# Four PSUM banks as one tile, v loaded and cast by GpSimd, and state by head pairs, in a fused RWKV and squared-ReLU kernel

## Chip, cores and metric

The kernel runs on one core of one Trainium2 chip. The metric is the device time in microseconds (us) of one execution. Three runs of the kernel before gave 177.93, 178.39 and 179.38 us; the median is 178.39 us.

The engines have short names in what follows: PE is TensorE (PEld its weight load), DVE is VectorE, ACT is ScalarE, POOL is GpSimd, SP is SyncE, which here only issues transfers. PSUM, into which PE writes, has eight banks; a bank holds 512 float32 values in each of 128 partitions.

## What is computed

```
def _attn_ref(r, k, v, w, u):                       # r, k, v: (4, 8, 768, 48); w, u: (8, 48)
    state = np.zeros((B, H, D, D), dtype=np.float32)
    for t in range(S):
        kt, vt, rt = (k[:, :, t].copy(), v[:, :, t].copy(), r[:, :, t].copy())
        cur = np.einsum('bhd,bhe->bhde', u[None] * kt, vt)
        y[:, :, t] = np.einsum('bhd,bhde->bhe', rt, state + cur)
        state = w[None, :, :, None] * state + np.einsum('bhd,bhe->bhde', kt, vt)
...
x = y as (3072, 384) tokens
h = x @ w_in                                        # w_in: (384, 2048)
g = np.maximum(h, 0.0) ** 2
out = g @ w_out                                     # w_out: (2048, 384)
```

First comes a linear attention with a decaying state (batch 4, 8 heads, 768 steps, head size 48), then two matrix products with a squared ReLU between them on its output.

## The kernel before

**Units.** The 768 steps are cut into 6 chunks of 128; a chunk of one batch is a unit, so there are 24 units (`units`, chunk outermost). Inside a unit the recurrence is written as matrices. r and k are multiplied by powers of w (`scale`, L321: tiles `wpos` and `wneg`, made from the logarithm of w at the start), which gives `rkw`. This is transposed to `rkT`: for the first 6 units by PE and ACT (`turn`, `evict_rk`), for the others by a transposing transfer on SP's queue (`turn_dma`, L330). From `rkT` come the scores of 128 by 128 for each head (`at`, L358, PE), which DVE masks and evicts (`mask`, L370). `sums` (PE, L378 and L383) makes the diagonal term from `rk` (the u part) and, in the same bank, the unit's new part of the state. `diag_v` (DVE, L392) multiplies the diagonal term by v. `state_add`, `state_decay` and `state_cast` (L400 to L412) update the state of the batch in float32 and leave a bfloat16 copy `stb`. `y_mm` (PE, L421 and L427) adds masked scores times v and r times the state; `evict_y` (DVE, L436) evicts this as `yb`, and it is transposed into `xT` (`x_turn` or `x_dma`).

**The two products.** `mm1` (PE, L468) multiplies `xT` by w_in, into one bank for each 512 values; a group takes one unit, or two units for six pairs in the middle (`GROUPS`), so that its matmuls are 128 or 256 wide. ACT evicts each bank with a ReLU (`relu`, L476, tile `gr`). The square is taken by ACT (`square`, L483) or DVE (L485), by the letters of `SQUARES` in turn. `mm2` (PE, L492) multiplies by w_out, four calls of four matmuls into one bank for a unit, and ACT evicts (`evict_o`, L499) before the store. The last unit does this in two halves (L508).

**State by heads.** The heads of a pair share the 128 partitions, 64 each. `sums` makes a block of 96 columns for a pair, of which only the two diagonal blocks are wanted; `state_add` and `state_cast` work on them one by one, in 64 partitions and 192 values each, and `stb` has its other blocks set to zero at the start.

**Order.** Nothing is ordered by the framework: the function declares each step with a cost, its needs, the buffers it takes and a rank (`Plan.add`), and `Plan.run` goes through them in a list schedule with these costs and writes out one program in order of the planned starts. The rank decides between steps that are ready. A PSUM bank is given to a step when the plan starts it (the bank that has been free longest), and fillers (`fill`, L276, matmuls of a constant) go into PE's queue where the plan has nothing for it in the first 16 us. The planned times are not in the program. What an engine waits for in the end are semaphores that are put in from the tiles that each instruction reads and writes: an instruction waits for those that stand before it in the written order and touch the same tile in a conflicting way. For PSUM two reads of a bank by two engines are also kept apart.

**Transfers.** Loads of r, k and v, the transposes and the stores go by SP's queue, in the plan's order; a transfer's semaphore is used again after eight transfers of its kind, and the later one waits for the earlier. The weights go by GpSimd's queue, which casts them to bfloat16; a one-element copy (`weights`, L306) that reads a loaded tile holds each of them back (`FRONT`). w is loaded once into all 128 partitions by ACT's queue, and once with u by GpSimd for the columns.

Of the kernel before, what the change touches and what calls it, by code (L numbers as in the profile page):

```python
# [16 lines left out]
class Plan:  # L17
# [9 lines left out]
    def __init__(self, lags, cold, spare):  # L27
        self.lags = lags
        self.cold = cold
        self.spare = spare  # L30
        self.steps = []
        self.at = {}
        self.users = {}
        self.place = {}

    def add(self, key, engine, cost, emit, needs=(), rank=0.0, new=(), uses=(), move=None):
        s = dict(key=key, engine=engine, cost=cost, emit=emit, rank=rank, new=new, move=move)
        s["needs"] = [n for n in needs if n is not None]
        self.at[key] = s
        self.steps.append(s)  # L40
        for x in tuple(new) + tuple(uses):
            self.users.setdefault(x, []).append(s)

    def run(self, room, banks, count):
# [10 lines left out]
        begin, until, tight, loose = self.spare  # L55
        held[0] = "spare"
        order = []
        t = 0.0
# [5 lines left out]
        def ready(s, e):  # L64
            if s["move"]:
                return s["end"] + moved
# [96 lines left out]
def kernel(  # L163
# [33 lines left out]
    loads = ctx.enter_context(tc.tile_pool(name="loads", bufs=6))  # L197
# [5 lines left out]
    banks = [psum.tile([128, 512], F32, name=f"bank{n}") for n in range(8)]  # L203
    plan = Plan((0.9, 0.0, 0.2, 0.33, 0.12), (5.5, 1.9), (1.25, 16.0, 0.057, 0.08))
# [20 lines left out]
    nc.vector.memset(warm, 1.0)  # L225
    wu = const.tile([HP, 2, 2, 64], F32)
# [3 lines left out]
    nc.gpsimd.dma_start(out=wu[:, 1, :, :D], in_=u.rearrange("(p o) d -> p o d", o=2))  # L230

# [6 lines left out]
    ident4 = const.tile([HP, HP], F32)  # L238
    make_identity(nc, ident4)
    lnw = const.tile([128, dm], F32)  # L240
# [3 lines left out]
    for wx, by in ((wpos, up), (wneg, down)):  # L244
        nc.scalar.activation(wx.rearrange("p h d -> p (h d)"), lnw, AF.Exp, scale=by)
# [4 lines left out]
    for n in range(NPAD):  # L250
        for x in range(2):
            nc.vector.memset(rkw_b[n][:, x, :, :, D:], 0.0)
# [8 lines left out]
    st32 = [const.tile([128, HP, D], F32, name=f"st32_{b}") for b in range(B)]  # L261
    stb = [const.tile([128, HP, 2 * D], BF16, name=f"stb_{b}") for b in range(B)]
    for b in range(B):
        nc.vector.memset(stb[b], 0.0)

    wend_c = const.tile([128, HP], F32)
    wend = wend_c.unsqueeze(2).to_broadcast([128, HP, D])
# [27 lines left out]

    def load(i, name):
        c, b = units[i]
        src = {"rt": r, "kt": k, "vt": v}[name]
        x = loads.tile([C, H, D], F32, name=name)
        nc.sync.dma_start(  # L300
            out=x, in_=src[b, :, c * C : (c + 1) * C, :].rearrange("h s d -> s h d")
        )
# [19 lines left out]

    def cast_v(i):
        tiles[i]["vb"] = work.tile([C, H, D], BF16, name="vb")
        nc.scalar.copy(tiles[i]["vb"], tiles[i]["vt"])  # L325

    def turn_dma(i):
        t = tiles[i]
        t["rkT"] = work.tile([128, 2, HP, C], BF16, name="rkT")
# [5 lines left out]
    def turn(i, x):  # L335
        t = tiles[i]
        t["tp", x] = bank("h", i, "rk", x).bitcast(BF16)[:, : HP * C].rearrange("p (a c) -> p a c", a=HP)
        if x == 0:
            t["rkT"] = work.tile([128, 2, HP, C], BF16, name="rkT")
# [54 lines left out]
    def state_add(i):  # L394
        c, b = units[i]
        for o in range(2):
            sl = slice(o * 64, o * 64 + 64)
            x = tiles[i]["s"][sl, :, o * D : (o + 1) * D]
            if c == 0:
                nc.vector.tensor_tensor(st32[b][sl], x, wend[sl], ALU.mult)  # L400
            else:
                nc.vector.tensor_tensor(st32[b][sl], x, st32[b][sl], ALU.add)  # L402
# [138 lines left out]
    add("w", ACT, 3.9, None, rank=-1e3)  # L541
    add("wk", ACT, 0.48, None, rank=-1e3, needs=["w"])
    copy("begin", SP, 0.74, None, rank=-1e3)
    add("wu", POOL, 4.6, None, rank=-1e3)
# [3 lines left out]
    add("wend", ACT, 0.4, end_columns, rank=10, needs=["copied"])  # L548
    for n, (what, q, gated) in enumerate(FRONT):
        copy(  # L550
            (what, q), POOL, 1.0, do(weights, gated, q, what), rank=n,
            move=((2.35, 98, 1.25, 0.0) if what == "I" else (2.05, 78, 1.25, 0.0)), needs=[gated], uses=[gated],
        )
    for i in range(NU):
# [4 lines left out]
        for n, name in enumerate(("rt", "kt", "vt")):  # L559
            copy(  # L560
                (name, i), SP, 0.55, do(load, i, name), rank=rank + 0.1 * n, move=(1.06, 16, 0.67, 1.0),
                new=[(name, i)],
            )
        for x in range(2):
# [5 lines left out]
        add(  # L570
            ("vb", i), ACT, 0.405, do(cast_v, i), rank=a + 0.5, needs=[("vt", i), ("rkT", i) if i < 24 else ("scale", i, 1)],
            new=[("vb", i)], uses=[("vt", i)],
        )
# [12 lines left out]
        else:  # L586
            copy(("rkT", i), SP, 1.24, do(turn_dma, i), rank=a - 30, needs=both, move=(1.5, 26, 0.67, 1.0), new=[("rkT", i)], uses=[("rkw", i)])
# [10 lines left out]
        for o in range(2):  # L598
# [7 lines left out]
            new=[("s", i)], uses=[("rk", i), ("rkw", i)] + ([("vb", i)] if c < NCH - 1 else []),  # L606
        )
        add(("dv", i), DVE, 0.465, do(diag_v, i), rank=a + 2, needs=[("sums", i), ("vb", i)], new=[("dv", i)], uses=[("s", i), ("vb", i)])
        if c < NCH - 1:
            add(  # L610
                ("sadd", i), DVE, 0.68, do(state_add, i), rank=a + (4 if c else 3.2),
                needs=[("sums", i), ("stb", before) if c else "wend"], uses=[("s", i)],
            )
            if c > 0:
                add(("sdec", i), DVE, 0.27, do(state_decay, i), rank=a + 4 + 4, needs=[("sadd", i)])
            add(
                ("stb", i), ACT, 0.71, do(state_cast, i), rank=a + 6 + 4,
# [5 lines left out]
            new=[("y", i)], uses=[("am", i, 0), ("am", i, 1), ("vb", i), ("rkT", i)],  # L623
# [8 lines left out]
        else:  # L632
            copy(("xT", i), SP, 1.2, do(x_dma, i), rank=a - 30, needs=xneed, move=(0.6, 26, 0.67, 0.4), new=xnew, uses=[("yb", i)] + xuse)
    begun = 0
    step = 0
    for m in GROUPS:
# [17 lines left out]
        for j in range(i, i + m):  # L654
            a = 4 * j
            squares = [[("sq", i, s) for s in range(q * m, q * m + m)] for q in range(NQ)]
            if j < NU - 1:
# [7 lines left out]
                copy(("out", j), SP, 0.42, do(store, j), rank=a + 4 + L2, needs=[("osb", j)], move=(0.58, 75, 0.67, 0.13), uses=[("osb", j)])  # L665
                continue
            for n in range(2):
# [9 lines left out]
                copy(("out", j, n), SP, 0.42, do(store_half, j, n), rank=a + 4 + L2, needs=[("osb", j, n)], move=(0.35, 75, 0.67, 0.13), uses=[("osb", j, n)])  # L677
    room = dict(
        rt=6, kt=6, vt=6, rkw=NPAD, g=2, rkT=4, vb=4, rk=4, am=8, dv=4, yb=4, xT=3, gr=6, osb=6,
    )  # L680
    for s in plan.run(room, dict(at=4, s=2, y=2, h=5, o=2), len(banks)):
# [32 lines left out]
```

## Time and profile before

| | us |
|---|---|
| median of 3 runs | 178.39 |
| profiled execution: its time | 179.7 |
| profiled execution: its span | 177.9 |
| PE busy | 167.5 |
| of it fillers | 11.9 |
| DVE busy | 128.7 |
| ACT busy | 128.8 |
| POOL busy | 11.4 |

The span is the time from the first to the last recorded instruction; 1.8 us of the profiled execution lie around it. A matmul's recorded time contains its way through the array, so that of 12 matmuls of 0.219 us that follow each other only about 0.056 us each are spent; a group's sum of busy time counts overlapping records once. In the rows by line, "mean ns of one" is the length of one instruction, and what stands behind the second bar is the time that the engine sat idle just before the instructions of that row, with what ended most of this. A stretch's row gives, after the length, the busy time of PE, PEld, DVE, ACT and POOL (instructions begun in it), then the clock granted to PE, the transfer engines' share and GB/s.

### The profile page before, as it was taken

What the parts mean: (1) busy time and instruction counts of PE and PEld (TensorE: products, weight loads), DVE (VectorE), ACT (ScalarE), POOL (GpSimd) and SP (SyncE); (2) the same over time, 40 slices, a digit from 0 to 9 for tenths busy, and PEclk for the clock granted to TensorE, in tenths of its full rate; (3) what the DMA queues carried; (4) which work ended last, traced back from release to release, by engine and by line L of the source; (5) the groups of instructions that cost most, each with busy time, mean ns of one, the idle gap of its engine ahead of it and who ended that gap; (6) DMA issues with size and microseconds to landing.
All of it is one profiled execution on the core that took longest, in us unless ns stands there. A gap on an engine that the chain in (4) does not pass through costs nothing.

```text
span 177.9 us, 5106 instructions
## 1 busy us (share of the span) xinstructions
PE 167.5 (94%) x2080; PEld 135.2 (76%) x2080; DVE 128.7 (72%) x279; ACT 128.8 (72%) x268; POOL 11.4 (6%) x35
## 2 busy tenths in 40 slices
PE   7699689999999999989979999899999999999993
PEld 7599479977786886876776796786795797878762
DVE  3389996565989899769779698589598695853100
ACT  2738889999385985597488599488597499659820
POOL 7120950000000000000000000000000000000000
PEclk9999999999999999999999999999999999999999
DMA  5999999999797888869879889999998897940212
GB/s 103 192 179 181 163 197 197 208 190 179 93 208 128 169 155 171 175 132 206 174 161 185 176 166 191 133 201 185 163 199 172 187 201 135 314 135 0 71 67 90
DMA packets 107385, 29.05 MB, mean 163 GB/s; under 512 B 101985, under 2 KB 106849, under 8 KB 107361
## 3 DMA queue, kind: packets, MB, share of 16 engines
q1 hardware_dynamic: 104976, 25.37, 75.1%
q0 software_dynamic: 2240, 3.15, 10.0%
q8 instruction: 16, 0.26, 0.6%
q10 hardware_dynamic: 144, 0.20, 0.6%
q14 instruction: 9, 0.07, 0.1%
HBM read 20.65 MB, written 4.72 MB: 143 GB/s over the span
## 4 chain that ended last, share of the span: by engine, by line
PE 57%; DMA 18%; DVE 17%; issue 3%; ACT 2%; SPq 1%; ACTq 0%
PE bank L492 22%; PE bank L468 22%; DMA rkT<-rkw 8%; DMA rt<-in_r_dram 5%; DVE am L370 4%; DVE rkw L321 4%; DVE yb L436 3%; PE bank L358 3%; DMA xT<-yb 2%; PE bank L276 2%; DMA wrow<-in_w_dram 2%; DVE dv L392 2%; DVE g L485 2%; PE bank L421 1%; PE bank L508 1%
## 5 line engine op out<-in xcount | busy, mean ns | idle before, releaser
L468 PE MATMUL bank<-xT,w_in_q 128*128 128x128 bf16 (+1 forms) x864 | 71.8, 237 | 0.5 <-ACT xT L456 0.3
L476 ACT ACTIVATE gr<-bank 128x512 f32<-128x512 f32 x96 | 55.0, 601 | 19.5 <-PE bank L468 18.9
L468 PEld LDWEIGHTS <-w_in_q 128*128 128x128 bf16 x864 | 64.4, 114 | 3.3 <-issue 0.7
L492 PE MATMUL bank<-w_out_q,g 128*128 128x384 bf16 x368 | 65.1, 326 | 0.0
L492 PEld LDWEIGHTS <-g 128*128 128x128 bf16 x368 | 34.4, 98 | 20.0
L370 DVE TENSOR_TENSOR am<-bank,smask 128x512 bf16<-128x512 f32 x48 | 31.8, 684 | 8.2 <-PE bank L358 8.1
L483 ACT ACTIVATE g<-gr 128x512 bf16<-128x512 f32 x60 | 37.3, 639 | 0.6
L485 DVE TENSOR_TENSOR g<-gr 128x512 bf16<-128x512 f32 x36 | 24.6, 687 | 13.1 <-ACT gr L476 13.0
L499 ACT COPY osb<-bank 128x384 f32<-128x384 f32 x23 | 11.0, 484 | 10.1 <-PE bank L492 7.9
L412 ACT CAST stb<-st 64x192 bf16<-64x192 f32 x40 | 14.0, 350 | 5.1 <-DVE st L406 4.4
L350 DVE TENSOR_TENSOR rk<-rkT 128x512 bf16<-128x512 bf16 x24 | 10.1, 422 | 7.7 <-DMA rkT<-rkw 5.6
L321 DVE TENSOR_TENSOR rkw<-rt,wpos 128x384 bf16<-128x384 f32 x24 | 13.2, 552 | 2.5 <-DMA rt<-in_r_dram 1.7
L436 DVE TENSOR_TENSOR yb<-bank,dv 128x384 bf16<-128x384 f32 x24 | 13.3, 555 | 2.3 <-PE bank L427 1.7
L392 DVE TENSOR_TENSOR dv<-vb,bank 128x384 f32<-128x384 bf16 x24 | 13.1, 545 | 2.6 <-PE bank L383 2.6
L321 DVE TENSOR_TENSOR rkw<-kt,wneg 128x384 bf16<-128x384 f32 x24 | 13.2, 551 | 0.6 <-DMA kt<-in_k_dram 0.3
L276 PE MATMUL bank<-warm 128*128 128x128 bf16 x108 | 11.9, 275 | 1.1 <-DVE warm L225 1.1
L358 PE MATMUL bank<-rkT 64*128 64x128 bf16 x192 | 9.8, 222 | 2.8 <-DMA rkT<-rkw 1.9
L325 ACT CAST vb<-vt 128x384 bf16<-128x384 f32 x24 | 12.2, 508 | 0.2
L402 DVE TENSOR_TENSOR st<-bank,st 64x192 f32<-64x192 f32 x32 | 11.3, 352 | 0.2
L358 PEld LDWEIGHTS <-rkT 64*128 64x128 bf16 x192 | 5.5, 96 | 7.5 <-issue 2.9
L276 PEld LDWEIGHTS <-warm 128*128 128x128 bf16 x108 | 9.6, 128 | 1.4 <-DVE warm L225 1.1
L345 ACT COPY rkT<-bank 128x512 bf16<-128x512 bf16 x12 | 6.9, 585 | 4.5 <-PE bank L341 4.5
(54 smaller groups left out, 97.8 us busy)
## 6 DMA issues: line engine op xcount, KB each, us to landing
rt<-in_r_dram SPq DMA_DIRECT2D x24, 192.0 KB, 4.2
kt<-in_k_dram SPq DMA_DIRECT2D x24, 192.0 KB, 4.0
vt<-in_v_dram SPq DMA_DIRECT2D x24, 192.0 KB, 4.4
out_dram<-osb SPq DMA_DIRECT2D x23, 192.0 KB, 2.8
w_in_q<-in_moe_w_in_dram POOLq DMA_DIRECT2D x4, 384.0 KB, 7.2
w_out_q<-in_moe_w_out_dram POOLq DMA_DIRECT2D x4, 384.0 KB, 13.1
rkT<-rkw SPq DMA_TRANSPOSE x18, 3.8
xT<-yb SPq DMA_TRANSPOSE x18, 3.0
```

The source lines that it names most:

```text
L276: nc.tensor.matmul(out=banks[0][:, :128], lhsT=warm, rhs=warm, start=True, stop=True)
L321: nc.vector.tensor_tensor(t["rkw"][:, x, :, :, :D], pair(src), pair(wx), ALU.mult)
L358: nc.tensor.matmul(out=t["at"][o][:, p, :], lhsT=t["rkT"][sl, 1, p, :], rhs=t["rkT"][sl, 0, p, :], start=True, stop=True,)
L370: nc.vector.tensor_tensor(am, t["at"][o], smask.unsqueeze(1).to_broadcast([C, HP, C]), ALU.mult)
L392: nc.vector.tensor_tensor(t["dv"], t["vb"], t["d"].unsqueeze(2).to_broadcast([C, H, D]), ALU.mult)
L412: nc.scalar.copy(stb[b][sl, :, o * D : (o + 1) * D], st32[b][sl])
L436: nc.vector.tensor_tensor(t["yb"], t["y"], t["dv"].rearrange("p h d -> p (h d)"), ALU.add)
L468: nc.tensor.matmul(out=t["h", s][:, a], lhsT=turned, rhs=chunks[c]["xT"][:, n, b : b + m, :], start=(n == 0), stop=(n == NK - 1),)
L476: nc.scalar.activation(t["gr", s], t["h", s], AF.Relu)
L483: nc.scalar.activation(g, x, AF.Square)
L485: nc.vector.tensor_tensor(g, x, x, ALU.mult)
L492: nc.tensor.matmul(out=t["o"], lhsT=chunks[units[i][0]]["g"][:, f, units[i][1], :], rhs=w_out_q[f // 4][:, f % 4, :], start=(f == 0), stop ...
```

## The change

- w's second load goes to four partitions (0, 32, 64 and 96), two heads each, instead of to 128. Its logarithm is taken there, and four matmuls with a row of ones (`spread_log`) spread it over all partitions, each into a bank of its own. The exponentials that make `wpos` and `wneg` read these four banks at once (`power`).
- For this, banks 4 to 7 are slices of one PSUM tile, `four`. After the start they are banks like the others, given out by the plan.
- v of units 6 to 23 is loaded and cast by GpSimd's queue (`load_v`, eight buffers `vc`). Units 0 to 5 keep SP's load and ACT's cast. These transfers stand behind the weights in GpSimd's queue.
- The state is kept with all its 96 columns for a pair. `wend`, the decay over a chunk, is a tile of 128 by 384 with zeros outside the diagonal blocks, which are filled by GpSimd at the start. Add, decay and cast are one instruction each.
- The zeros that pad `rkw` are set by GpSimd for all but two buffers; there are 8 buffers for `rkw` instead of 5, 6 instead of 4 for `rkT`, 7 instead of 6 for the loads.
- `SQUARES` has six of eight on ACT instead of five; the weights' gates differ; a table `TURNS` gives single steps a rank of their own, so that the whole order differs.

```
+    def add(self, key, ...):
+        kind, which = (key[0], key[1] if len(key) == 2 else key[1:]) if isinstance(key, tuple) else ("", key)
+        rank = self.turns.get(kind, {}).get(which, rank)
...
-                                n = min((n for n in held if held[n] is None), key=lambda n: since[n])
+                                n = 4 + x[1] if x[0] == "log" else min((n for n in held if held[n] is None), key=lambda n: since[n])
...
-    NPAD = 5
-    SQUARES = 'AMAMAAAM'
+    NPAD = 8
+    NVB = 8
+    SQUARES = 'AAAMAAAM'
+    TURNS = {
+        "rt": {
+            0: -49.089, 1: -33.297, 10: 12.513, 12: 23.673, ...
+        },
+        ...
+    }
     FRONT = (
-        ("I", 0, ("kt", 1)), ("I", 1, ("kt", 3)), ("I", 2, ("kt", 3)), ("O", 0, ("kt", 3)),
-        ("I", 3, ("kt", 3)), ("O", 1, ("kt", 3)), ("O", 2, ("kt", 3)), ("O", 3, ("kt", 3)),
+        ("I", 0, ("vt", 0)), ("I", 1, ("kt", 2)), ("I", 2, ("vt", 1)), ("O", 0, ("kt", 3)),
+        ("I", 3, ("kt", 4)), ("O", 1, ("kt", 4)), ("O", 2, ("rt", 4)), ("O", 3, ("rt", 4)),
     )
...
-    banks = [psum.tile([128, 512], F32, name=f"bank{n}") for n in range(8)]
+    four = psum.tile([128, 4, 512], F32, name="four")
+    banks = [psum.tile([128, 512], F32, name=f"bank{n}") for n in range(4)] + [four[:, n] for n in range(4)]
...
-    wrow = const.tile([128, dm], F32)
-    nc.scalar.dma_start(out=wrow, in_=w.rearrange("h d -> (h d)").unsqueeze(0).to_broadcast([128, dm]))
+    wrow = const.tile([128, 2 * D], F32)
+    nc.gpsimd.memset(wrow, 1.0)
+    nc.scalar.dma_start(out=wrow[::32], in_=w.rearrange("(a o) d -> a (o d)", o=2))
...
-    for wx, by in ((wpos, up), (wneg, down)):
-        nc.scalar.activation(wx.rearrange("p h d -> p (h d)"), lnw, AF.Exp, scale=by)
...
+    def spread_log():
+        for a in range(HP):
+            sl = slice(a * 32, a * 32 + 1)
+            nc.tensor.matmul(out=four[:, a, : 2 * D], lhsT=ones[sl], rhs=lnw[sl], start=True, stop=True)
+
+    def power(out, by):
+        nc.scalar.activation(out.rearrange("p (a o) d -> p a (o d)", o=2), four[:, :, : 2 * D], AF.Exp, scale=by)
...
+    def end_blocks():
+        for o in range(2):
+            sl = slice(o * 64, o * 64 + 64)
+            nc.gpsimd.tensor_copy(wend[sl, :, o * D : (o + 1) * D], wend_c[sl].unsqueeze(2).to_broadcast([64, HP, D]))
...
+    def load_v(i):
+        c, b = units[i]
+        tiles[i]["vb"] = work.tile([C, H, D], BF16, name="vc", bufs=NVB)
+        nc.gpsimd.dma_start(out=tiles[i]["vb"], in_=v[b, :, c * C : (c + 1) * C, :].rearrange("h s d -> s h d"))
...
     def state_add(i):
         c, b = units[i]
-        for o in range(2):
-            sl = slice(o * 64, o * 64 + 64)
-            x = tiles[i]["s"][sl, :, o * D : (o + 1) * D]
-            if c == 0:
-                nc.vector.tensor_tensor(st32[b][sl], x, wend[sl], ALU.mult)
-            else:
-                nc.vector.tensor_tensor(st32[b][sl], x, st32[b][sl], ALU.add)
+        nc.vector.tensor_tensor(st32[b], tiles[i]["s"], st32[b] if c else wend, ALU.add if c else ALU.mult)
...
     def state_cast(i):
         b = units[i][1]
-        for o in range(2):
-            sl = slice(o * 64, o * 64 + 64)
-            nc.scalar.copy(stb[b][sl, :, o * D : (o + 1) * D], st32[b][sl])
+        nc.scalar.copy(stb[b], st32[b])
...
-        add(
-            ("vb", i), ACT, 0.405, do(cast_v, i), rank=a + 0.5, needs=[("vt", i), ("rkT", i) if i < 24 else ("scale", i, 1)],
-            new=[("vb", i)], uses=[("vt", i)],
-        )
+        if i < NPE:
+            add(
+                ("vb", i), ACT, 0.405, do(cast_v, i), rank=a + 0.5, needs=[("vt", i), ("rkT", i)],
+                new=[("vb", i)], uses=[("vt", i)],
+            )
+        else:
+            copy(("vb", i), POOL, 1.1, do(load_v, i), rank=a + 50, needs=[("kt", i - 1)], move=(1.06, 16, 1.4, 0.0, LATE[0]), new=[("vc", i)])
```

More of the change, by code (lines that the diff above doesn't have):

```diff
@@ L225 @@
     nc.vector.memset(warm, 1.0)
+    ones = const.tile([128, 128], F32)
+    nc.vector.memset(ones, 1.0)
     wu = const.tile([HP, 2, 2, 64], F32)
@@ L249 @@
     rkw_b = [const.tile([128, 2, HP, 2, 64], BF16, name=f"rkw{n}") for n in range(NPAD)]
-    for n in range(NPAD):
-        for x in range(2):
-            nc.vector.memset(rkw_b[n][:, x, :, :, D:], 0.0)
+    for n in range(2):
+        nc.vector.memset(rkw_b[n][:, :, :, :, D:].rearrange("p x a o e -> p (x a o) e"), 0.0)
     identb = const.tile([128, 128], BF16)
@@ L328, in turn_dma @@
         t = tiles[i]
-        t["rkT"] = work.tile([128, 2, HP, C], BF16, name="rkT")
+        t["rkT"] = work.tile([128, 2, HP, C], BF16, name="rkT", bufs=6)
         nc.sync.dma_start_transpose(
@@ L338, in turn @@
         if x == 0:
-            t["rkT"] = work.tile([128, 2, HP, C], BF16, name="rkT")
+            t["rkT"] = work.tile([128, 2, HP, C], BF16, name="rkT", bufs=6)
         for p in range(HP):
@@ L539 @@
     plan.fill = fill
[L541 to L544, printed above, removed]
+    add("w0", ACT, 2.55, None, rank=-1e3)
+    add("log", PE, 0.25, spread_log, rank=-1e3, needs=["w0"], new=[("log", n) for n in range(4)])
+    add("w", ACT, 0.48, do(power, wpos, up), rank=-1e3, needs=["log"], uses=[("log", n) for n in range(4)])
+    add("wk", ACT, 0.48, do(power, wneg, down), rank=-999, needs=["w"], uses=[("log", n) for n in range(4)])
+    add("wu", POOL, 5.8, None, rank=-1e3)
     add("cols", PE, 0.1, spread_columns, rank=-50, needs=["wu"], new=[("h", "cols")])
@@ L547 @@
     add("uwb", POOL, 0.75, u_columns, rank=-200, needs=["copied"])
-    add("wend", ACT, 0.4, end_columns, rank=10, needs=["copied"])
+    add("end", ACT, 0.4, end_columns, rank=0, needs=["copied"])
+    add("wend", POOL, 0.8, end_blocks, rank=1.5, needs=["end"])
     for n, (what, q, gated) in enumerate(FRONT):
@@ L586 @@
         else:
[L587 removed]
+            copy(("rkT", i), SP, 1.24, do(turn_dma, i), rank=a - 30, needs=both, move=(1.5, 26, 0.67, 1.0, LATE[1]), new=[("rkT", i)], uses=[("rkw", i)])
         add(("rk", i), DVE, 0.335, do(rk, i), rank=a + 1, needs=[("rkT", i)], new=[("rk", i)], uses=[("rkT", i)])
@@ L676 @@
                 )
-                copy(("out", j, n), SP, 0.42, do(store_half, j, n), rank=a + 4 + L2, needs=[("osb", j, n)], move=(0.35, 75, 0.67, 0.13), uses=[("osb", j, n)])
+                copy(("out", j, n), SP, 0.42, do(store_half, j, n), rank=a + 4 + L2, needs=[("osb", j, n)], move=(0.35, 75, 0.67, 0.13, 0.0), uses=[("osb", j, n)])
     room = dict(
-        rt=6, kt=6, vt=6, rkw=NPAD, g=2, rkT=4, vb=4, rk=4, am=8, dv=4, yb=4, xT=3, gr=6, osb=6,
+        rt=7, kt=7, vt=7, rkw=NPAD, g=2, rkT=6, vb=6, vc=NVB, rk=4, am=8, dv=4, yb=4, xT=3, gr=6, osb=6,
     )
-    for s in plan.run(room, dict(at=4, s=2, y=2, h=5, o=2), len(banks)):
+    for s in plan.run(room, dict(at=4, s=2, y=2, h=5, o=2, log=4), len(banks)):
         if s["emit"] is not None:
```

127 lines of the change are left out of this document (100 added, 27 removed), and 16 rows, old and new, of the table TURNS.

## The prediction

> **What bounds the kernel now.** I read the summary first, then the chain that ended last, the stretches in time, and last the rows of the tiles that the change touches.
>
> ```profile
> span 177.9 us, 5106 instructions
> ...
> PE 167.5 (94%) x2080; PEld 135.2 (76%) x2080; DVE 128.7 (72%) x279; ACT 128.8 (72%) x268; POOL 11.4 (6%) x35
> ...
> PE   7699689999999999989979999899999999999993
> ...
> PEclk9999999999999999999999999999999999999999
> ...
> PE 57%; DMA 18%; DVE 17%; issue 3%; ACT 2%; SPq 1%; ACTq 0%
> ```
>
> TensorE (PE) is the bound: 94% busy and most of the chain. ACT and DVE are each at 72%, so work taken from them is worth nothing by itself. What can be gained is PE's idle time and its filler matmuls. The stretches show where these lie (length, then PE, PEld, DVE, ACT, POOL busy):
>
> ```profile
> 5.00:10.00 5.00, 3.78 (x36) 3.31 (x36) 2.18 (x5) 3.06 (x7) 0.78 (x4) 1.00 1.21 192
> ...
> 15.00:20.00 5.00, 4.21 (x83) 3.64 (x81) 4.94 (x11) 4.12 (x9) 1.95 (x4) 1.00 0.94 182
> 20.00:25.00 5.00, 3.74 (x72) 3.02 (x70) 4.94 (x12) 4.41 (x10) 4.68 (x11) 1.00 1.09 169
> 25.00:30.00 5.00, 4.93 (x91) 4.58 (x88) 4.00 (x9) 4.90 (x11) 0.00 (x0) 1.00 1.17 197
> ...
> 85.00:90.00 5.00, 3.98 (x57) 3.27 (x57) 3.03 (x8) 2.61 (x5) 0.00 (x0) 1.00 0.93 197
> ...
> 115.00:120.00 5.00, 4.07 (x51) 3.80 (x49) 3.91 (x8) 4.37 (x10) 0.00 (x0) 1.00 0.99 214
> ```
>
> To 25 us DVE is full and PE waits for it; from 25 us PE is full but for a few gaps (1.02 in 85 to 90, 0.93 in 115 to 120, 0.55 in 75 to 85, 0.37 in 125 to 140: 2.9 us; the chain has transposes `rkT<-rkw` there). So from 25 us on, **any wait put into PE's stream is added to the time.** This is why PE's waits matter most below. The rows for prices:
>
> ```profile
> L476 ACT ACTIVATE gr<-bank 128x512 f32<-128x512 f32 x96 | 55.0, 601 | 19.5 <-PE bank L468 18.9
> L483 ACT ACTIVATE g<-gr 128x512 bf16<-128x512 f32 x60 | 37.3, 639 | 0.6
> L370 DVE TENSOR_TENSOR am<-bank,smask 128x512 bf16<-128x512 f32 x48 | 31.8, 684 | 8.2 <-PE bank L358 8.1
> L485 DVE TENSOR_TENSOR g<-gr 128x512 bf16<-128x512 f32 x36 | 24.6, 687 | 13.1 <-ACT gr L476 13.0
> L499 ACT COPY osb<-bank 128x384 f32<-128x384 f32 x23 | 11.0, 484 | 10.1 <-PE bank L492 7.9
> L392 DVE TENSOR_TENSOR dv<-vb,bank 128x384 f32<-128x384 bf16 x24 | 13.1, 545 | 2.6 <-PE bank L383 2.6
> L325 ACT CAST vb<-vt 128x384 bf16<-128x384 f32 x24 | 12.2, 508 | 0.2
> L402 DVE TENSOR_TENSOR st<-bank,st 64x192 f32<-64x192 f32 x32 | 11.3, 352 | 0.2
> ```
>
> **Work on ACT and DVE.** 18 casts of v go: 18 x 0.508 = 9.1 us off ACT. Squares go from 60 on ACT and 36 on DVE to 72 and 24: 12 x 0.639 = 7.7 onto ACT, 12 x 0.687 = 8.2 off DVE. The state add, two of 64x192 (0.73 a pair on the timeline), becomes one of 128x384 (0.545, by `dv`): 20 x 0.18 = 3.6 off DVE; the decay grows from 0.350 to 0.55 (as `rkw<-rt,wpos`, 128x384): 16 x 0.20 = 3.2 on; the state cast from a pair at 0.72 to one at 0.51: 4.2 off ACT. ACT falls to about 123 us, DVE to about 119. Priced at 0: PE's own work hides it; if DVE's 8.6 us all lay in the first 25 us it would be worth that, but only four state adds (0.7) do.
>
> **Start.** Before, w's 192 KB land 3.64 us after issue, Ln takes 0.52, and `wpos` ends at 5.56. After: a memset on POOL that ACT's queue waits for (to 0.95), a w of 1.5 KB, a shorter Ln, four fp32 matmuls that PE's queue waits for (two smaller ones, L281, took 0.49 together), an exponential of the same size (0.6). With the fastest small transfer of this trace (1.5, the last store) `wpos` is ready at 4.3; with 3.64, a full 0.52 and 1.0 of matmuls at 6.8. I take 2.0 for the transfer: 4.8, so **-0.8**, between -1.3 and +1.3. Queued behind PE's wait are the fillers and the first transposes, which need the same result.
>
> **v by GpSimd.** SP issues 18 transfers fewer (median 0.95 each). The same bytes are read, so DMA time is put at 0. POOL's issues took 0.56 (w_out) to 0.77 (w_in, 384 rows); by rows a v of 1024 would take up to 2.1: 10 to 37 us on an engine that is empty from 25 us. With 8 buffers a v is issued as soon as the unit eight earlier is done with its own; only unit 6 is close, since its v stands behind the last w_out (issued 24.2, 14.7 at most to land: 38.9; plus 4.4 for a v: 43.3; in before its matmuls begin at 44.9). 0, up to +3 if cover fails; late next would be PE's `sums` and `y` of unit 6. Deeper pools (rkT 6, rkw 8) and the freed SP queue should take away the 2.9 us of gaps above: **-2.9**, between 0 and -2.9.
>
> **One tile for four banks.** This is the part that decides. Banks 4 to 7 become slices of one tile `four`. I followed each wait in the changed program to the instruction that raises the semaphore to the awaited value. In the program before, no engine waits for another over a bank that it does not use. In the changed one this happens often: 70 waits of PE on ACT or DVE, 63 between ACT and DVE, 63 of these two on PE, where the only thing shared is `four` and the banks differ. One stretch, unit 9 (lines of the changed kernel; m2 is L596, mask L482, `vc` a v that GpSimd loads):
>
> ```
> PE   L572 m1, writes four bank 0, 12 matmuls     raises PE to 908
> ACT  L580 relu, reads four bank 2                waits PE 908        raises ACT to 97
> PE   L490 diag, writes four bank 3               waits ACT 97
> ```
>
> The relu's own matmuls were done earlier, yet it starts only when the next group is through, and PE stands until it ends. A turn like this costs PE: the matmul's tail after the pitch (0.219 - 0.056 = 0.16), 0.03 to the reader's start, the reader, and 0.06 back (`rkT` ends at 21.76, L358 starts at 21.82): 0.85 with a relu (0.60), 0.93 with a mask (0.68), 0.80 with `dv`, 0.73 with `osb`, less the PE work that stands between. With pitches from the chain (m1 0.67 for 12, wide m1 2.62 for 24, m2 0.65 for 4, L358 0.33 for 8) I did this sum for every wait of PE behind the fillers. One reader deep: 33 stalls, 18.3 us. Two deep, where the reader itself waits for the other engine's reader, as `dv` for a relu for a mask: 43 stalls, 26.8 us. Three deep: 49 stalls, 32.5 us. By the same sum the kernel before has 2 stalls, 1.0 us. ACT's and DVE's own queues, which add to this, are left out. I take the middle of two and three deep, 29.6 - 1.0 = **+28.6**, from which 1.5 at the front lies in PE's idle time there: **+27.1**.
>
> **Sum**: 27.1 - 0.8 - 2.9 = +23.4. The profiled execution took 179.7 (span 177.9, 1.8 around it), 1.3 over the median of 178.39. 179.7 + 23.4 = 203.1 for such an execution; about **202** for the median.
>
> **Rivals.**
> - Half-absorbed: PE's queue stands, but DVE and ACT get ahead, so that only single turns remain. For it: both have 50 us of room. Against: 14 of these stalls have no PE work at all in between. 18.3 - 1.0 - 1.5 - 0.8 - 2.9 = +12.1: 190. Chance 0.14.
> - ACT and DVE take turns: with 63 waits between them, late masks and relus also delay `y` and xT. If every second one costs a further 0.6: 31 x 0.6 = 19 on top: 221. For it: DVE is full to 25 us; against: both have room later. 0.12.
> - The other side: the readers have always finished by the time that PE arrives, since relus waited 18.9 us for PE, not PE for them. Then the start and the gaps remain: 178.4 - 3.7 = 174.7. It decides if fewer than some 4 of the turns stall (3.7 / 0.85). Against: the relu above cannot begin until PE has issued its last matmul. 0.05. [...]
> - The clock falls: PE's short stops bring its clock down. If a third of 165 us of PE work ran at half pace: +55 on top: 257. Against: in 20 to 25 us PE was busy 3.74 of 5 and PEclk stayed at 1.00. 0.03. [...]
>
> **Chances.** The forecast 0.66, the rivals 0.14, 0.12, 0.05, 0.03. No change to 1% (about what a measurement of this kernel can tell) lies only at the edge of the other side: faster 0.04, same 0.01, slower 0.95. The range runs from the half-absorbed case (190, less 1) to three deep with half of the second rival's 19 and nothing gained (178.4 + 31.5 + 9.5 = 219): 189 to 219.
>
> **What would show it.** PE's row busy share falls to the low eighties or lower, with idle time before m1, m2 and diag matmuls of tile `four` released by ACT L580 and DVE L482, some 40 times, 0.5 to 0.9 us each; ACT relus on `four` that begin when a matmul of another bank ends; DVE near 119 and ACT near 123 us. `wpos` ends before 5.56. No wait for `vc` but perhaps unit 6. It is wrong if PE stays above 90% busy from 30 us on, or if the lost time is before `vc` or `rkT` transfers.

## The result, and the profile after

The changed kernel takes 217.84 us (median of four runs, 214.92 to 220.25) against 178.54 for the kernel before in the same rounds: a ratio of 1.214, interval 1.201 to 1.228. It is slower by 39 us. The forecast was 202, with a range of 189 to 219. Some executions of a kernel took longer than its others, a slow state; ratios, their intervals and the differences in us below leave these out, while medians and ranges hold all. The profiled execution took 217.9 us, its span is 216.1.

The summary and the chain that ended last, from the page of the kernel after:

```profile
span 216.1 us, 5059 instructions
...
PE 176.4 (82%) x2088; PEld 137.4 (64%) x2088; DVE 121.1 (56%) x236; ACT 125.4 (58%) x242; POOL 29.7 (14%) x63
...
PE   5976786898987786987787987987998786989894
...
PEclk9999998899996999999999999999999999999999
...
PE 62%; DVE 16%; ACT 15%; issue 3%; DMA 1%; POOL 0%; DVEq 0%; ACTq 0%; POOLq 0%
```

PE does much the same work, but its busy share is down from 94% to 82%, and the stops are spread over the whole span: 11 of the 40 slices in the row of PE are at 90% or more, where 32 were before. DVE (121.1 us) and ACT (125.4) did less than before, as worked out, and gained nothing by it. In the chain, transfers fell from 18% to 1%, and ACT rose from 2% to 15%: the program now ends last because PE, ACT and DVE wait for each other. PEclk dips twice (8 8, and later 6), which it did not do in the profiled execution of the kernel before. The four executions had mean clocks of 0.984, 0.969, 0.984 and 1.00; the one at 1.00 still took 214.92 us, so that the clock is worth some 3 us of the 39.

The groups by line of the kernel after (after the counts: busy us, mean ns of one, idle time before, and what ended it), one line for matmuls into own banks and one for the same matmuls into `four`:

```profile
L596 PE MATMUL bank<-w_out_q,g 128*128 128x384 bf16 x240 | 45.4, 329 | 0.0
L572 PE MATMUL four<-xT,w_in_q 128*128 128x128 bf16 (+1 forms) x486 | 44.8, 242 | 13.1 <-ACT gr L580 5.9 <-DVE yb L540 3.1 <-DVE st L508 1.7
L572 PE MATMUL bank<-xT,w_in_q 128*128 128x128 bf16 (+1 forms) x378 | 33.5, 240 | 0.6 <-ACT xT L560 0.6
L596 PE MATMUL four<-w_out_q,g 128*128 128x384 bf16 x128 | 23.9, 325 | 8.1 <-DVE am L482 5.5 <-ACT gr L580 1.4 <-DVE dv L504 1.1
...
L490 PE MATMUL bank<-uwb,rk 128*128 128x8 bf16 x48 | 3.0, 169 | 0.0
L490 PE MATMUL four<-uwb,rk 128*128 128x8 bf16 x48 | 3.0, 167 | 4.1 <-DVE am L482 3.2 <-ACT gr L580 0.9
```

This is the clearest view of the cause. The same line, with the same operands, waits 13.1 us where it writes a slice of `four` and 0.6 where it writes a bank with a tile of its own; for m2 8.1 against 0.0, for the diagonal term 4.1 against 0.0. What ends these waits has nothing to do with the matmul: m2 (L596) never reads what the mask (L482) makes. In the list of PE's waits (us in total, times, longest):

```profile
PE four L572 <- ACT gr L580: 5.9, 10, 1.4
PE four L596 <- DVE am L482: 5.5, 6, 1.4
PE four L490 <- DVE am L482: 3.2, 3, 1.6
PE four L572 <- DVE yb L540: 3.1, 4, 1.3
```

The whole list has 44 waits of PE on ACT or DVE before a matmul of `four`, 32.2 us together, 0.73 each. The readers wait too, for matmuls and for each other:

```profile
ACT gr L580 <- PE four L572: 14.4, 17, 2.2
...
ACT gr L580 <- DVE dv L504: 5.3, 3, 3.2
...
DVE dv L504 <- ACT gr L580: 4.2, 4, 2.1
DVE am L482 <- ACT gr L580: 4.1, 4, 2.6
```

The first of these rows says little, since relus stood 18.9 us for their own matmuls in the kernel before; the other three have no counterpart there.

Last the chain from 113.66 us, in order of time (start, length, what):

```profile
113.66 0.83 PE four L572 x6
114.51 0.61 ACT gr L580
115.12 0.04 issue
115.16 0.83 PE four L572 x6
116.02 0.60 ACT gr L580
116.61 1.04 ACT g L587 x2
```

In the chain six matmuls into `four`, a relu, six matmuls, a relu follow each other, 1.5 us a pair. PE's own rows in this stretch (in brackets the idle time before, and what ended it):

```profile
113.66 0.82 PE L572 MATMUL four<-xT,w_in_q 128*128 128x256 bf16 x6
114.41 0.40 PE L470 MATMUL bank<-rkT 64*128 64x128 bf16 x8
115.16 0.82 PE L572 MATMUL four<-xT,w_in_q 128*128 128x256 bf16 x6 [0.35 <-ACT gr L580]
115.81 0.24 PE L490 MATMUL bank<-uwb,rk 128*128 128x8 bf16 x4
115.92 0.33 PE L495 MATMUL bank<-vc,rkw 128*128 128x96 bf16 x4
116.66 0.82 PE L572 MATMUL four<-xT,w_in_q 128*128 128x256 bf16 x6 [0.41 <-ACT gr L580]
```

Short matmuls into other banks fill a part of each relu's 0.6 us, and PE stands for the rest, 0.35 and 0.41 us.

### The profile page after: what moved, and what is told of

Same layout as the page of the kernel before. It is cut to its first block, busy times and chain, and to the rows that moved or that the text cites. A ratio compares the mean times of both kernels' runs of the same rounds, so it can differ in the third digit from the quotient of the medians.

```text
span 216.1 us, 5059 instructions
## 1 busy us (share of the span) xinstructions
PE 176.4 (82%) x2088; PEld 137.4 (64%) x2088; DVE 121.1 (56%) x236; ACT 125.4 (58%) x242; POOL 29.7 (14%) x63
## 3 DMA queue, kind: packets, MB, share of 16 engines
q1 hardware_dynamic: 86256, 21.83, 55.7%
## 4 chain that ended last, share of the span: by engine, by line
PE 62%; DVE 16%; ACT 15%; issue 3%; DMA 1%; POOL 0%; DVEq 0%; ACTq 0%; POOLq 0%
PE four L572 17%; PE bank L596 15%; PE four L596 10%; ACT gr L580 10%; DVE am L482 7%; PE bank L572 6%; DVE yb L540 3%; DVE st L508 2%; DVE dv L504 2%; PE bank L372 2%; ACT g L587 2%; PE four L470 1%; DMA wrow<-in_w_dram 1%; PE bank L470 1%; ACT rkT L457 1%
## 5 line engine op out<-in xcount | busy, mean ns | idle before, releaser
L580 ACT ACTIVATE gr<-four 128x512 f32<-128x512 f32 x54 | 31.8, 598 | 42.6 <-PE four L572 14.4
L572 PE MATMUL four<-xT,w_in_q 128*128 128x128 bf16 (+1 forms) x486 | 44.8, 242 | 13.1 <-ACT gr L580 5.9
L596 PEld LDWEIGHTS <-g 128*128 128x128 bf16 x368 | 34.5, 98 | 28.7 <-issue 10.2
L596 PE MATMUL bank<-w_out_q,g 128*128 128x384 bf16 x240 | 45.4, 329 | 0.0
L572 PE MATMUL bank<-xT,w_in_q 128*128 128x128 bf16 (+1 forms) x378 | 33.5, 240 | 0.6 <-ACT xT L560 0.6
L596 PE MATMUL four<-w_out_q,g 128*128 128x384 bf16 x128 | 23.9, 325 | 8.1 <-DVE am L482 5.5
L433 POOL DMA_DIRECT2D vc<-in_v_dram x18 | 15.8, 888 | 93.0 <-PE four L531 44.0
L482 DVE TENSOR_TENSOR am<-four,smask 128x512 bf16<-128x512 f32 x27 | 18.5, 690 | 15.7 <-ACT gr L580 4.1
L580 ACT ACTIVATE gr<-bank 128x512 f32<-128x512 f32 x42 | 24.5, 598 | 4.4 <-PE bank L572 4.3
L482 DVE TENSOR_TENSOR am<-bank,smask 128x512 bf16<-128x512 f32 x21 | 14.0, 686 | 9.2 <-PE bank L470 8.1
L428 DVE TENSOR_TENSOR rkw<-rt,wpos 128x384 bf16<-128x384 f32 x24 | 13.1, 551 | 2.0 <-ACT wpos L380 2.0
L516 ACT CAST stb<-st 128x384 bf16<-128x384 f32 x20 | 10.2, 509 | 6.8 <-DVE st L512 6.7
L428 DVE TENSOR_TENSOR rkw<-kt,wneg 128x384 bf16<-128x384 f32 x24 | 13.1, 551 | 0.0
```

The costliest lines, as they stand in the source:

```text
L428: nc.vector.tensor_tensor(t["rkw"][:, x, :, :, :D], pair(src), pair(wx), ALU.mult)
L433: nc.gpsimd.dma_start(out=tiles[i]["vb"], in_=v[b, :, c * C : (c + 1) * C, :].rearrange("h s d -> s h d"))
L482: nc.vector.tensor_tensor(am, t["at"][o], smask.unsqueeze(1).to_broadcast([C, HP, C]), ALU.mult)
L516: nc.scalar.copy(stb[b], st32[b])
L572: nc.tensor.matmul(out=t["h", s][:, a], lhsT=turned, rhs=chunks[c]["xT"][:, n, b : b + m, :], start=(n == 0), stop=(n == NK - 1),)
L580: nc.scalar.activation(t["gr", s], t["h", s], AF.Relu)
```

## The experiments

Two theories stood at the start. **The tile**: nearly all of the loss comes from the waits that one tile for four banks brings. **The order**: the searched ranks, or v by GpSimd, or the start cost as much. When the first runs showed that the rest of the change cost something as well, the later ones took that apart.

**1. A tile for each bank.** The changed kernel with eight tiles; the exponentials become four for each of `wpos` and `wneg`.

```
-    four = psum.tile([128, 4, 512], F32, name="four")
-    banks = [psum.tile([128, 512], F32, name=f"bank{n}") for n in range(4)] + [four[:, n] for n in range(4)]
+    banks = [psum.tile([128, 512], F32, name=f"bank{n}") for n in range(8)]
```

> The changed kernel, order and all, but banks 4 to 7 are four tiles of their own; the start's exponentials read them bank by bank (eight short ones for two). Theory (PE, ACT and DVE stand in turns because a wait is put in for any bank of the shared tile): nearly the whole loss goes, and what is left is the start and the closed gaps: 178.5 - 3.7 + about 1 for the eight exponentials, 174 to 178; PE over 92% busy, clock 1.00 throughout. Rival A (the searched order, or v by GpSimd, or the wider state work is the loss): it stays above 205. Rival B (half and half): 185 to 205.

Measured: 183.72 us (181.55 to 184.83); ratio to the kernel before 1.017, interval 1.009 to 1.026. With the same program otherwise, 35 of the 39 us are gone (217.8 to 182.3). The tile is the cause, and in the profiled execution (181.55 us) PE's row and clock are back; in the other three the mean clock was 0.979 to 0.988 and the time 1.6 to 3.3 us longer:

```profile
PE 166.8 (93%) x2088; PEld 133.1 (74%) x2088; DVE 118.5 (66%) x236; ACT 122.3 (68%) x248; POOL 30.3 (17%) x63
...
PEclk9999999999999999999999999999999999999999
```

But 174 to 178 was expected, and this kernel is 3.3 us above the kernel before (4.7 by the medians of all runs, the figure that the expectation of 5 starts from). The rest of the change costs, where the prediction had it gain 3.7.

**2. Two tiles of two banks.** As 1, but banks 4 and 5 are slices of one tile, 6 and 7 of another.

```
+    two = [psum.tile([128, 2, 512], F32, name=f"two{n}") for n in range(2)]
+    banks = [psum.tile([128, 512], F32, name=f"bank{n}") for n in range(4)] + [two[n // 2][:, n % 2] for n in range(4)]
```

> The changed kernel with banks 4 to 7 as two tiles of two banks. Theory: a bank shares its tile with one other instead of three. The same sum of turns as in the prediction gives 4.3 us three deep (18 stalls at most) for 32.5 with one tile of four, so 5 to 8 us over the kernel with tiles of its own: 180 to 184. Rival (any sharing of a PSUM tile costs the same, or the loss is elsewhere): 205 or more. Rival (the waits are harmless): as with tiles of its own.

Measured: 185.70 us (184.73 to 187.20), ratio 1.037, interval 1.030 to 1.044: 3.4 us over own tiles, where four banks in one cost 35 and 5 to 8 was expected. PE stood 19 times for ACT or DVE, 10.3 us together, against 10 times and 6.4 us with own tiles. The price does not grow evenly with the number of shared banks. A likely reason, not tested apart, is that with two in a tile there is only one other bank whose reader can stand in the way.

**3. The kernel before with one tile for four banks.** Nothing else of the change.

```
-    banks = [psum.tile([128, 512], F32, name=f"bank{n}") for n in range(8)]
+    four = psum.tile([128, 4, 512], F32, name="four")
+    banks = [psum.tile([128, 512], F32, name=f"bank{n}") for n in range(4)] + [four[:, n] for n in range(4)]
```

> The kernel before, with nothing changed but that banks 4 to 7 are slices of one tile. Theory: the loss comes with the tile alone; the sum of turns in this order is 19.3 us three deep, less 1.0 that it had; measured losses ran some 1.3 times the sum in the changed kernel, so 178.5 + 18 to 25: 196 to 204. Rival (the tile costs only with the new order): 178 to 181.

Measured: 216.91 us (215.16 to 218.51), ratio 1.207, interval 1.199 to 1.215. Two lines of the source, which change no instruction's work, cost the kernel before 38 us. The page:

```profile
PE 179.2 (83%) x2080; PEld 140.0 (65%) x2080; DVE 131.0 (61%) x279; ACT 131.6 (61%) x268; POOL 10.3 (5%) x35
...
PEclk9997856999999999999999999999999999967999
```

196 to 204 was expected from a sum of turns of 19 us: the cause is confirmed, and the size is missed by half. In the list of PE's waits on ACT and DVE 37 stand before `four`, 26.3 us together, 0.71 each. Against the page of the kernel before, PE's idle time is 25.4 us longer and its busy time, in which tails (37 x 0.16 = 5.9) and clock lie, 11.7; together this is 37.1, the difference of the spans. The mean clock is 0.952, so that 0.048 x 215 = some 10 us of clock were lost. Little of that is time: another execution, with a mean clock of 0.984, took 215.16 us against 217.11, 2 us less for 7 us of clock. That the clock would fall belonged to a rival; it falls here, and it is a small part of the loss.

**4. Own tiles without the searched ranks.** As 1, with `TURNS = {}`.

> As the changed kernel with tiles of its own, but with an empty table of ranks, so the order is the one that the declared ranks give. It tells what the searched order itself is worth. Theory: 1 to 6 us worse than the searched order with tiles of its own, since the order was of use and is not the loss: 176 to 183. Rival (the order is the loss): faster than with the searched order.

Measured: 183.05 us (181.29 to 184.32), ratio 1.018, interval 1.011 to 1.026. This is 3.6 us over the kernel before, where kernel 1 is 3.3; 1 to 6 us worse than kernel 1 was expected. The ranks are worth nothing that can be measured here, and they are not what kernel 1 loses.

**5. Own tiles, v of all units by SP.** As 1, without `load_v`; SP loads every v and ACT casts it.

```
-        for n, name in enumerate(("rt", "kt", "vt") if i < NPE else ("rt", "kt")):
+        for n, name in enumerate(("rt", "kt", "vt")):
```

> The kernel with eight own banks (183.7 us), but v of all units by SP's queue and cast by ACT, as before the change. What is asked: where the 4.7 us above the kernel before (179.05) come from. Theory (v by GpSimd): eight v are issued in one burst from 27.4 us, their casting packets hold the transfer engines longer (29.1% of the engines' time for 20960 packets, against 71.2% for 86256 of SP's), so that k of one unit took 8.8 us to land and transposes into xT 4.2 instead of 3.0. Then this kernel is at 178 to 180.5, and PE's losses at 45 to 60 us (3.49, 4.31, 4.74 of 5) go. Rival (the rest of the change: start, gates of the weights, letters of the squares, order): it stays at 182.5 or above, and the slices at 45 to 60 us stay as they are. ACT gets 18 casts back: 122.3 + 9.1 = 131.4 busy.

Measured: 191.79 us (189.03 to 193.94), ratio 1.070, interval 1.062 to 1.077. The theory had 178 to 180.5: a miss, and on the side of the rival. This kernel is 12.2 us over the kernel before and kernel 1 only 3.3, so that in this plan v by GpSimd is worth some 9 us. Why is not shown whole: in front of transposes (L444) SP stood 8.4 us for m1 on PE (L574), against 2.1 in kernel 1, and 9.4 for `rkw`, against 8.0; at 140 to 145 us PE worked only 2.61 of 5 us, and behind it the clock fell to 0.50 (0.66 in the mean from 145 to 150 us).

**6. Own tiles, 3 buffers for v instead of 8.**

> Eight own banks, v of units 6 on by GpSimd as in the changed kernel, but 3 buffers for it instead of 8, so that a v is not issued before the unit three earlier is done with its own. It tells the burst from the packets. If the burst of eight at 27 to 35 us is the cost: 179.5 to 181.5. If the dearer packets are the cost wherever they lie, or if v has nothing to do with it: 183 to 185. If v now comes late: above 185, with PE idle before sums or y released by vc.

Measured: 188.09 us (186.84 to 191.76), ratio 1.056, interval 1.051 to 1.062. It tells nothing of the burst: no engine waited for a late `vc`, but the number of buffers enters the plan, and PE lost 4.2 us before L497 to `vb` of the first units, whose v landed 10.4 us (median) after issue instead of 6.7. The clock fell behind this stop (mean 0.970 over the profiled execution).

**7. The kernel before with v by GpSimd.** `load_v` and its 8 buffers for units 6 on; nothing else of the change.

> The kernel before with one thing changed: v of units 6 to 23 by GpSimd's casting queue into 8 buffers. Theory (v by GpSimd costs): 181.5 to 184. Rival (the rest of the change costs): 178 to 180. By the prediction's term (0, up to -2.9 for the freed SP queue): 176 to 179.

Measured: 183.43 us (182.37 to 185.63) against 178.19, ratio 1.035, interval 1.029 to 1.041: 5.2 us slower, with no `four` in it. This is more than the 3.3 that were left over in 1, but it cannot simply be taken as their cause: in that plan v by SP cost more still (5). Its stretches (length, PE, PEld, DVE, ACT, POOL busy, clock, transfer engines' share, GB/s):

```profile
40.00:45.00 5.00, 5.00 (x64) 3.75 (x63) 1.72 (x4) 4.67 (x9) 0.00 (x0) 1.00 1.84 135
45.00:50.00 5.00, 4.49 (x48) 2.70 (x46) 3.96 (x8) 1.08 (x2) 0.00 (x0) 1.00 1.72 137
50.00:55.00 5.00, 2.79 (x35) 2.13 (x32) 1.99 (x4) 3.57 (x8) 0.00 (x0) 1.00 1.48 141
```

and the wait behind it:

```profile
PE bank L364 <- DMA rkT<-rkw: 2.3, 1, 2.3
```

In the kernel before, the share in the same stretches is 0.84, 1.02 and 1.10 and PE is busy all 5 us. Here it is up to 1.84, and at 52.8 us PE stops 2.3 us for a transposing transfer. (The GB/s, 135 to 141 against 160, 124 and 187, count a v that is cast at 96 KB, half of what is read, and do not say that less was read.) The spans of the two profiled executions differ by 2.6 us with the same busy time of PE, 167.5; between 45 and 55 us PE stops 2.7. The trace places the stop beside the burst but does not price it: in the kernel before PE stood for such transposes too, 1.9 us, later on. The queues, kind by kind (packets, MB, share of 16 engines' span), of the kernel before and then of this one:

```profile
q1 hardware_dynamic: 104976, 25.37, 75.1%
q0 software_dynamic: 2240, 3.15, 10.0%
```
```profile
q1 hardware_dynamic: 86256, 21.83, 69.2%
q0 software_dynamic: 20960, 4.92, 28.4%
```

By these rows the 18 v (18,720 packets) add 0.284 x 16 x 180.5 - 0.10 x 16 x 177.9 = 536 us of engine time to GpSimd's queue, and SP's queue, with as many packets fewer, loses only 139. A cast packet took 29 ns of an engine, where the mean of SP's packets in the kernel before is 20; but those that stay in SP's queue rise to 23 here (0.692 x 16 x 180.5 / 86,256), so that a part of a packet's time goes with the load.

**8. The same with 3 buffers for v.** The kernel of 7, `NVB = 3`.

> The kernel before with v of units 6 on by GpSimd's casting queue, as in the run of 183.4 us, but into 3 buffers instead of 8. v by GpSimd alone cost 5.2 us there; PE lost 2.2 of 5 us at 50 to 55 us, behind a stretch in which six v lay in the queue at once (transfer engines' share 1.84 and 1.72 at 40 to 50 us). Theory (the burst costs): with three at most in flight the loss at 45 to 55 us goes, 179 to 181. Rival (the packets cost wherever they lie, 28.4% of the engines' time for 4.9 MB): 182.5 to 185. Above 186: v comes late or the order in SP's queue no longer fits.

Measured: 180.49 us (179.41 to 182.20) against 179.31, ratio 1.013, interval 1.005 to 1.021. This is 2.0 us over, where 8 buffers cost 5.2: some three fifths of the cost of v goes when no more than three transfers can be in flight. In its trace PE is busy all 5 us in each of the three stretches from 40 to 55 us, at a share of 1.44, 1.17 and 0.96. So the burst is the likely larger part; since the number of buffers enters the plan as well, it is not shown apart from the order. What remains is not separated: the dearer packets would explain it, and in the profiled execution (182.20, the longest of the six) PE also stood 2.7 us for `w_in_q`, and behind it the clock fell to 0.50 (0.66 in the mean from 25 to 30 us).

**9. The kernel before with the state by pairs.** One add, one decay and one cast of 128x384; `wend` filled by GpSimd.

```
+        nc.vector.tensor_tensor(st32[b], tiles[i]["s"], st32[b] if c else wend, ALU.add if c else ALU.mult)
...
+        nc.scalar.copy(stb[b], st32[b])
```

> The kernel before with one thing changed: the state with all 96 columns of a pair, one add, one decay and one cast each, and its decay tile filled by GpSimd. DVE 128.7 - 3.6 + 3.2 = 128.3 busy, ACT 128.8 - 4.2 = 124.6. PE is the bound, so 178 to 180, no measurable difference; 177 or less would mean that the casts by halves stood on PE's path; above 181 that the decay tile, ready later at the start, holds up the first state adds and so the banks of the sums.

Measured: 178.74 us against 178.19, ratio 1.007, interval 1.003 to 1.011. ACT is at 123.5 us and DVE at 126.8, five and two less than before, and the time does not fall: at 72% these engines had room. The 0.7% that it lost is more than its interval; the cause was not looked for.

**10. The kernel before with deeper pools.** `rkw` 8, `rkT` 6, `vb` 6, loads 7; the zeros of six `rkw` by GpSimd.

> The kernel before with the pools of the changed one: 8 buffers rkw, 6 rkT, 6 vb, 7 for the loads, the zeros of six rkw by GpSimd. By the prediction's term (gaps of 2.9 us behind rkT transfers go): 175.5 to 177. Rival: the gaps hang on SP's order and on the transfer engines, not on the buffers: 178 to 180, or more where loads that start earlier take the engines from the transposes.

Measured: 179.30 us against 179.31, ratio 1.005, interval 0.999 to 1.011. The rival holds as far as the time goes. In the trace the stretches that the prediction named lose 0.7 us instead of 2.9, but 100 to 105 us, full before, now loses 1.3: closed in one place, a gap opens in another.

**11. The kernel before with w in four partitions,** into four tiles of their own.

> The kernel before with the changed start alone: w to four partitions, its logarithm spread by four matmuls, into four tiles of their own, read by four exponentials each for wpos and wneg. By the prediction's term 177 to 178.5 (wpos ready at 4.8 instead of 5.56). By the trace of the changed kernel (wpos at 5.72, the small transfer took 3.0 us) and two times four small exponentials instead of two large: wpos and wneg 0.5 to 1 later, 178.5 to 180.

Measured: 178.97 us against 179.31, ratio 0.998, interval 0.991 to 1.004. No gain and no loss.

**12. Own tiles, v by SP, and no ranks.** The kernel of 5 with `TURNS = {}`.

> The kernel of 191.8 us (eight own banks, v of all units by SP) with the table of ranks emptied. Theory: that kernel was slow because its order in SP's queue was made for a queue without v; SP stood 9.4 us before the transposing transfers for rkw and 8.4 for PE. Then without the table it comes to 178.5 to 182. Rival (the gates of the weights, the letters of the squares and the deeper pools cost by themselves): it stays above 186.

Measured: 186.44 us (185.65 to 187.67), ratio 1.048, interval 1.041 to 1.056. 178.5 to 182 was expected: a miss, on the side of the rival. The ranks made some 4 of the 12 us of kernel 5, so its order was part of it; 8 remain. In the trace one stop holds most of them. SP's queue (start, length of the issue, what):

```profile
24.54 7.31 SPq L323 DMA_DIRECT2D vt<-in_v_dram  x1
31.89 3.21 SPq L323 DMA_DIRECT2D rt<-in_r_dram  x1
```
```profile
30.00:35.00 5.00, 0.00 (x0) 0.00 (x0) 0.00 (x0) 2.06 (x5) 0.00 (x0) 0.68 1.09 197
35.00:40.00 5.00, 3.81 (x52) 3.67 (x52) 3.62 (x8) 2.05 (x4) 0.00 (x0) 0.64 0.89 168
```

The issue of one v lasted 7.3 us; the r behind it was issued at 31.89 (DVE waited up to 8.0 us for an r); PE had nothing from 30 to 35 us and then a low clock. Whether the weights, five of which are issued from 18.9 to 26.7 here, or the letters of the squares brought the v into this place was not tried and stays open.

No version was faster than the kernel before.

## Why the prediction was right, and where it was not

**The mechanism was right.** It is the waits between different banks of one tile, in both directions. What was to show it is there: PE's busy share 82% ("low eighties"), 44 stops ("some 40") of 0.73 us ("0.5 to 0.9"), released by L580 and L482 first, DVE at 121 and ACT at 125 (119 and 123 were worked out). Experiments 1 and 3 show it from both sides: the tile taken from the changed kernel gives 35 us back, the tile alone put into the kernel before takes 38.

**"One tile for four banks" was mis-sized: +27.1 forecast, 35 measured.** The number of stops was right (43 at two deep, 49 at three, 44 found). The price of one was not. The sum charged 26.8 / 43 = 0.62 to 32.5 / 49 = 0.66, since it took off the PE work that lies between a matmul and the reader that it waits for. The trace shows 0.73 of idle time, and with the tail of 0.16 that the prediction put into each turn 0.89: on the mean as much as a full single turn, 0.85 to 0.93. (Against kernel 1, the span of the profiled executions is 36.3 longer: PE's idle time by 26.7, since some of these stops stand where PE would have stopped anyway, and its busy time by 9.6, in which tails and clock lie.) This is not because nothing was hidden: the two stops at 115 and 116 us are of 0.35 and 0.41, while the longest in the list are 1.4 to 1.6. Where a reader itself came late, the stop grew; the sum had left out ACT's and DVE's own queues, and said so. The rows of ACT and DVE above show such readers: `gr` stood 5.3 us for `dv`, and `dv` 4.2 for `gr`. How much of the difference each part makes is not shown. For kernel 3 the same sum gave 18 us (19.3 less 1.0) where 38 were measured, so that it is luck in part that 217.8 lies inside the range, whose upper end had been widened by half of a rival's 19.

**The three small gains were wrong in sign together: -3.7 forecast, +3.3 measured in kernel 1.** With the 8 us above, this is nearly the whole distance from 202 to 217.8.
- "v by GpSimd", 0: the failed step. It took DMA time as the bytes and found no late `vc`, and indeed no engine waits for `vc`. But many v go out close together (six back to back from 26.8 us in the changed kernel, eight from 24.3 to 39.8 in kernel 7), and what comes late in 7 is the others' transfers: DVE stood 2.5 us for k, where 0.3 before, and PE 2.3 for one transpose. The prediction's bound of +3 was tied to cover for v itself, the wrong victim. Alone it costs 5.2 us, with three buffers 2.0. What makes up the 3.3 of kernel 1 stays open all the same, since 5 shows that v by SP costs more in that plan.
- "Deeper pools and the freed SP queue", -2.9: 10 shows 0 for the pools, with gaps that moved. The freed queue shows no gain in 7, whose loss is larger.
- "Start", -0.8: it came out at 0. ACT's rows of the kernel after (start, length):

```profile
0.94 1.08 ACTq L319 DMA_DIRECT2D wrow<-in_w_dram  x1
...
3.98 0.28 ACT L340 ACTIVATE lnw<-wrow 128x96 f32<-128x96 f32 x1 [0.65 <-DMA wrow<-in_w_dram]
5.14 0.58 ACT L380 ACTIVATE wpos<-four,up 128x384 f32<-128x384 f32 x1 [0.88 <-PE four L377]
```

w of 1.5 KB landed 3.0 us after its issue, where 2.0 was assumed and 192 KB had taken 3.64; the four matmuls lie between 4.32 and 5.08, and `wpos` at 5.72, against 5.56 before. A small transfer saves little of such a latency, and the spread takes back what it saves. The bound of +1.3 held.

**"Work on ACT and DVE", priced 0**, was right: 9 moves the state alone and the time does not fall.

**The rivals.** The other side, with readers always done in time, is out: 35 us come and go with the tile alone. The half-absorbed case, 190, is out as well. "ACT and DVE take turns", 221, lies nearest the measured time, for a part of its reason: readers do wait for each other, which makes some turns longer than a single one. The falling clock was put at +55 (a third of PE's work at half pace, the author's estimate, which no run shows) and is real, but small: it is the two dips in PEclk. By microsecond (PE busy, count, clock, transfers' share, GB/s):

```profile
32.00:33.00 1.00, 0.16 (x4) 1.00 1.15 179
33.00:34.00 1.00, 0.51 (x12) 1.00 1.54 153
34.00:35.00 1.00, 0.00 (x0) 1.00 1.58 128
35.00:36.00 1.00, 0.84 (x8) 1.00 1.66 135
36.00:37.00 1.00, 1.00 (x7) 0.51 1.94 135
37.00:38.00 1.00, 1.00 (x19) 0.50 2.44 139
38.00:39.00 1.00, 1.00 (x15) 0.50 2.43 145
39.00:40.00 1.00, 1.00 (x17) 0.79 1.76 137
```

The clock halves at 36.0 us, after 3.4 us in which PE worked 1.5 us, and is whole again 3.4 us later. One such fall loses 0.49 + 0.50 + 0.50 + 0.21 = 1.70 us of clock; this kernel has two, 3.4 us, and they are part of the 35.

## What to carry to other kernels

Where semaphores are made from tiles, a tile is the unit of waiting (35 us here for four banks in one): never make one tile of buffers that different engines fill and drain in turn only because one instruction at the start would like to see them together. A transfer that is not on the path can still delay those that are (2.3 us for one transpose in kernel 7); before moving loads to another queue, count how many may be in flight at once. A limit by buffers can help (kernel 8, 2.0 us over the kernel before instead of 5.2), but where the buffers enter the plan it can cost as well (kernel 6, a ratio of 1.056 instead of 1.017). And when stops are counted from the program's semaphores, ask for each whether its reader can come late itself: the mean price here was that of a full turn, 0.89 us, though PE's other work filled a part of some.

## What the runs showed of the hardware that was not expected

- PE's clock fell to 0.50 and came back by itself. From the clock of single microseconds, the falls of the changed kernel last from 36.02 to 39.42 and from 66.74 to 70.14 us, 3.40 us each, and one each in kernels 5 and 8 from 145.20 to 148.62 and from 25.62 to 29.04. In kernel 3 the clock was lower for longer: 0.57, 0.50 and 0.91 in the three stretches of 5 us from 25 to 40 us, with more dips near 20 and 190 us in its PEclk row. In the 3.40 us before its two falls PE worked 1.53 and 1.50 us in the changed kernel; in kernel 5 it worked 0.65 us from 142 to 145 us. Not every stretch with as little work brings a fall: PE had 1.51 us of work from 14.5 to 17.9 us in the changed kernel and 0.80 from 52 to 55 us in kernel 7, and the clock stayed at 1.00. What decides is not shown.
- Casting packets in GpSimd's queue took some 29 ns of a transfer engine each in kernel 7, and the engines' share rose to 1.84 (0.84 from 40 to 45 us in the kernel before); the packets left in SP's queue rose from a mean of 20 ns to 23.
- Two slices in a tile cost 3.4 us and four cost 35, with the same order of work.
